# Block-sparse attention and a squared-ReLU MLP in one kernel: the second batch by gathered blocks, more transposes on TensorE, w_in products for pairs of token tiles

## The chip, the cores and the metric

The kernel runs on one core of a Trainium2 chip. The metric is the device time of one execution in microseconds, lower is better. The engines are TensorE (PE; its weight loads are listed apart as PEld), VectorE (DVE), ScalarE (ACT), GpSimd (POOL) and SyncE (SP), which in this kernel does nothing but issue DMAs. Each engine runs its own instructions in the order in which they stand; a semaphore makes one wait for another.

## The reference

Attention over 4 batches, 8 heads, 768 positions of 64 numbers, with a mask by blocks of 32 positions: each of the 24 query blocks sees its neighbours, the first and the last block, and three random blocks of its own; the first and last query block see everything. What comes out, 3072 tokens of 512 numbers, goes through a layer of 2048 with a squared ReLU:

```python
scores = scale * np.matmul(q, k.transpose(0, 1, 3, 2))
mask = np.abs(blk_i - blk_j) <= 1
mask = mask | (blk_i == 0) | (blk_j == 0) | (blk_i == 23) | (blk_j == 23)
for qb in range(24):
    for kb in sampled_blocks[qb]:       # three blocks a row
        mask[qb*32:(qb+1)*32, kb*32:(kb+1)*32] = True
attn = softmax(np.where(mask, scores, -1e9))
x = np.matmul(attn, v).transpose(0, 2, 1, 3).reshape(3072, 512)
r = np.maximum(x @ w_in, 0.0)           # 512 x 2048
return (r * r) @ w_out                  # 2048 x 512
```

Inputs and output are float32. The kernel casts to bf16 for TensorE.

## The kernel before

**Two ways of attention.** A unit is a pair of heads of one batch, 16 in all, four to a batch. Batches 0 and 1 (`SB = 2`) are dense: `attend` takes a unit and 256 queries, in three steps of 256 keys. Each step is `scores` (line 343, on TensorE), `exps` (line 357, one exponential of 128x1024 on ScalarE) and, for most, `masks` (line 363, a product on VectorE with a 0/1 tile `MK` which `mask_tile` and `mask_evac` build on TensorE and VectorE). For the first 256 queries of batch 0 there is no product: TensorE adds rows of minus infinities to the scores (`add` in line 343). Then come `values` or `values_full` (lines 372 and 389) and `normalize` (line 406).

Batches 2 and 3 are sparse. A `visit` (line 887) takes 128 query positions of all eight heads, as two groups of 64, and looks only at the blocks that the groups see. It needs the keys of the random blocks gathered in SBUF (`k_gather`, line 584: copies on POOL or VectorE whose addresses are block numbers in registers), and the values of those blocks gathered from a copy in DRAM: `v_store` (line 537) writes one batch's values as rows, `v_gather` (line 574) reads them back, through an indirect DMA on POOL or DMAs with register addresses on SP, and `v_window` (line 544) reads the neighbours and the edge blocks. Then `s_scores`, `s_exps` (line 620), `s_masks` (line 626), `s_values` (line 632; its matmuls stand at line 653 and go by column halves of TensorE, 128x64), and `s_normalize` (line 656). Two visits make 256 tokens.

A table tells which blocks to gather: `table_places`, `table_slots` (line 475) and `table_rows` build it on POOL and VectorE, `table_masks` makes the masks `MKS` of the gathered blocks, and `load_blocks` (its loads are line 561) brings block numbers into registers of POOL, VectorE and SP, all in one place.

**Transposes.** TensorE wants queries and keys, and later the attention's output, with the 64 or 128 features on the partitions. Queries and keys of batch 0 are transposed on TensorE (`transp`, copied out of PSUM by `evac`), those of the other batches by a transposing DMA on SP (`transp_dma`, line 311). The outputs of batch 0 go over TensorE (`x_transp`, `x_evac`), those of batch 1 and of the visits by DMA (lines 440 and 666).

**The MLP.** Twelve tiles of 256 tokens (`xT`, features on the partitions, `XT_BUFS = 4` in SBUF). For each, four times: `hidden` (line 681) multiplies four chunks of 128 of `w_in` with 256 tokens in four parts of eight matmuls; `relu` (line 697, ScalarE or VectorE), `square` (line 713, ScalarE, POOL or VectorE) follow. `output` (line 736) multiplies the squares with `w_out`, 512 wide; `out_copy` and `store` bring the result to DRAM.

**Halves of TensorE.** Nearly all matmuls have 64 rows of weights, one half of the array. `pair` (lines 201 to 203) issues two, one for each row half, which run together:

```python
def pair(out, lhsT, rhs, crossed=False, **kw):
    for r, rows in enumerate(HALVES):
        last = nc.tensor.matmul(out(r ^ crossed), lhsT(r ^ crossed, rows), rhs(r ^ crossed, rows), skip_group_check=True, **kw)
    return last.ins
```

Every such matmul is line 203 of the profile, so its groups are told apart by their tiles: `X<-xT,w_in_sb` is `hidden`, `X<-w_out_sb,g` is `output`, `X<-QKT` and `X<-QKT,KG` are scores, `X<-VB,pT` are values. `X` is PSUM, four slots of 128x2x512 (`NX = 4`).

**The order.** Each step above is a task, numbered as it is created. A table of words, `PROGRAM` (line 1001), lists all 1224 in the order in which they are issued, each with the engine that gets it (P, V, A, G for POOL, S) and, for a task that takes a PSUM slot, the slot: `P463/2` would be task 463 on TensorE into slot 2. `run_program` (line 92) goes through it; buffers are handed out in turn. So the order on each engine is written out by hand in that table and nothing reorders it.

**Loads.** `load` (line 145) brings a unit's queries, keys and values to raw buffers (three for queries, two each for keys and values), through SP, behind a gate on the weights' arrival. `cast_qk` and `cast_v` make bf16 of them; copies and casts of all engines are line 123.

## Time and profile before

| | us |
|---|---|
| three runs: lowest, median, highest | 261.82, 262.56, 263.5 |
| the profiled execution | 258.88 |
| its span on the core (first to last work) | 257.1 |
| granted clock of TensorE, mean | 1.00 |
| DMA: bytes moved, mean rate | 47.08 MB, 183 GB/s |
| POOL: squares (line 720), 20 of | 31.6, mean 1.587 each |
| POOL: indirect gathers of values (line 579), 19 of | 20.2, mean 1.061 each |
| ScalarE: ReLU (line 707), 28 of | 29.8, mean 1.068 each |
| VectorE: ReLU (line 709), 20 of | 24.5, mean 1.224 each |

The page of the profile gives for each engine the time in which it did work; register loads, semaphores and DMA issues are not counted in it. The groups of a line and a tile follow, with the busy time of all, the mean of one in ns, and the idle time just before them with what ended it. The profiled execution is 3.68 us shorter than the median of the three runs (1.4%), and 2.94 shorter than the lowest of them; where times are taken apart below, it is that execution.

Line numbers are those of the kernel before. In the changed kernel the same operations stand lower: the register loads at 580 for 561, copies at 125 for 123, the store of values at 557 for 538, the window's DMAs at 571 and 575 for 552 and 556, the indirect gathers at 598 for 579, the key gathers at 612 to 618 for 593 to 599, the squares at 754 for 720.

### The profile page before, as it was taken

How to read it: one execution, taken by the hardware profiler on the slowest of the kernel's cores; microseconds unless marked ns; L12 is line 12 of the kernel's file. 1: busy time of each engine (PE TensorE's matmuls, PEld its weight loads, DVE VectorE, ACT ScalarE, POOL GpSimd, SP SyncE). 2: the span in 40 equal slices, each digit the busy share in tenths (PEclk: the TensorE clock that was granted, in tenths of full speed). 3: DMA queues.
4: the chain of work that ended last, by engine and by line, in shares of the span. 5: the costliest groups of instructions: out<-in, count | busy, mean ns of one | idle time of the engine just before them, and what ended most of it. 6: DMA issues, size and time to landing. Idle time of an engine off the chain costs nothing.

```text
span 257.1 us, 12061 instructions
## 1 busy us (share of the span) xinstructions
PE 243.1 (95%) x5265; PEld 182.1 (71%) x5265; DVE 171.3 (67%) x408; ACT 183.6 (71%) x217; POOL 98.8 (38%) x178
## 2 busy tenths in 40 slices
...
GB/s 200 374 250 207 206 205 155 270 202 252 250 281 179 197 202 153 340 229 154 188 243 202 194 174 167 251 214 199 129 206 95 189 40 60 5 121 148 23 86 83
DMA packets 64692, 47.08 MB, mean 183 GB/s; under 512 B 31567, under 2 KB 60624, under 8 KB 64640
## 3 DMA queue, kind: packets, MB, share of 16 engines
...
## 4 chain that ended last, share of the span: by engine, by line
PE 53%; DVE 5%; DVEq 1%; issue 1%; ACT 1%; ACTq 0%
PE X L203 49%; PE X L653 4%; DVE VB L123 1%; ACT pT L623 1%; DVEq L561 1%; DVE MKS L123 1%; DVE pT L630 1%; DVE r L709 0%; DVE KG L599 0%; DVE qc L123 0%; DVE XS L413 0%; DVE KG L593 0%; DVE XS L662 0%; DVEq L599 0%; DVE rs L410 0%
## 5 line engine op out<-in xcount | busy, mean ns | idle before, releaser
L203 PE MATMUL X<-xT,w_in_sb 64*128 64x256 bf16 x1536 | 100.8, 269 | 2.8 <-issue 1.5
L203 PE MATMUL X<-w_out_sb,g 64*128 64x512 bf16 (+3 forms) x960 | 95.2, 334 | 0.1
L203 PEld LDWEIGHTS <-w_in_sb 64*128 64x128 bf16 x1536 | 74.6, 94 | 16.0 <-issue 5.4
L360 ACT ACTIVATE pT<-X 128x1024 bf16<-128x1024 f32 x72 | 70.6, 1030 | 7.6 <-PE X L203 6.8
L623 ACT ACTIVATE pT<-X 128x768 bf16<-128x768 f32 (+1 forms) x56 | 41.6, 766 | 26.5 <-PE X L203 23.9
L203 PEld LDWEIGHTS <-g 64*128 64x128 bf16 x960 | 40.3, 94 | 26.3 <-PE X L203 0.4
L720 POOL TENSOR_TENSOR g<-r 128x1024 bf16<-128x1024 f32 (+1 forms) x20 | 31.6, 1587 | 64.4 <-ACT r L707 47.2
L707 ACT ACTIVATE r<-X 128x1024 f32<-128x1024 f32 x28 | 29.8, 1068 | 20.6 <-PE X L203 20.5
L709 DVE TENSOR_SCALAR r<-X 128x1024 f32<-128x1024 f32 x20 | 24.5, 1224 | 26.7 <-PE X L203 13.7
L367 DVE TENSOR_TENSOR pT<-pT,VG 128x1024 bf16<-128x1024 bf16 x60 | 40.9, 715 | 0.2
L718 ACT ACTIVATE g<-r 128x1024 bf16<-128x1024 f32 (+1 forms) x40 | 35.2, 899 | 2.7 <-DVE r L709 2.5
L203 PE MATMUL X<-QKT 64*128 64x256 bf16 (+1 forms) x384 | 31.6, 250 | 3.3 <-DVE XS L413 1.3
L630 DVE TENSOR_TENSOR pT<-pT,MKS 128x768 bf16<-128x768 bf16 (+1 forms) x48 | 27.6, 607 | 10.7 <-ACT pT L623 10.5
L203 PEld LDWEIGHTS <-QKT 64*128 64x128 bf16 x384 | 16.7, 95 | 9.5 <-issue 4.1
L579 POOL DMA_INDIRECT VG<-rows,idx x19 | 20.2, 1061 | 4.4 <-issue 2.6
L203 PEld LDWEIGHTS <-pT 64*128 64x128 bf16 x768 | 16.0, 94 | 1.9
L203 PE MATMUL X<-VB,pT 64*128 64x65 bf16 x768 | 17.1, 190 | 0.0
L203 PEld LDWEIGHTS <-KG 64*128 64x128 bf16 x528 | 13.8, 95 | 4.5 <-issue 0.2
L659 DVE RECIPROCAL ss<-X 128x8 f32<-128x8 f32 x12 | 2.5, 206 | 19.5 <-PE X L653 17.3
L653 PEld LDWEIGHTS <-pT 128*64 128x64 bf16 x624 | 11.9, 111 | 4.9 <-issue 3.7
L203 PE MATMUL X<-QKT,KG 64*128 64x64 bf16 x528 | 15.3, 190 | 0.1
L123 POOL CAST VB<-vs 128x768 bf16<-128x768 f32 x9 | 7.8, 869 | 16.5 <-DMA vs<-in_v_dram 16.4
(107 smaller groups left out, 210.3 us busy)
## 6 DMA issues: line engine op xcount, KB each, us to landing
...
```

What stands on the lines that cost most here:

```text
L123: (V if e == "DVE" else G).tensor_copy(out=out, in_=in_)
L203: last = nc.tensor.matmul(out(r ^ crossed), lhsT(r ^ crossed, rows), rhs(r ^ crossed, rows), skip_group_check=True, **kw)
L360: A.activation(out=pT[:, :, 0:n], in_=stile.pop(a)[:, :, 0:n], func=AF.Exp, scale=scale)
L367: V.tensor_tensor(out=pT, in0=pT, in1=m[:, None].broadcast_to([P, 2, len(cs), w]), op=AOP.mult)
L579: G.indirect_dma_start(out=to[0:RS * HB], out_offset=None, in_=pairs, in_offset=bass.IndirectOffsetOnAxis(ap=idx[0:RS * HB, g - 1:g], axis=0))
L623: A.activation(out=pT[:, :, 0:n], in_=stile.pop((u, v, gs))[:, :, 0:n], func=AF.Exp, scale=scale)
L630: V.tensor_tensor(out=pT, in0=pT, in1=m[:, None].broadcast_to([P, 2, n]), op=AOP.mult)
L653: nc.tensor.matmul(po[i * D:(i + 1) * D, h, a * VW:(a + 1) * VW], pts[g][:, h, c * D:(c + 1) * D], val, start=a == 0 and c == 0, stop=c == ...
L707: A.activation(out=to, in_=src, func=AF.Relu)
L709: V.tensor_scalar(out=to, in0=src, scalar1=0.0, scalar2=None, op0=AOP.max)
L718: A.activation(out=g, in_=r, func=AF.Square)
L720: (G if e == "POOL" else V).tensor_mul(out=g, in0=r, in1=r)
```

## The change

Five things change together.

Batch 1 is sparse too (`SB` 2 to 1): six visits more, 18 in all, and a third store of values as rows. Only batch 0 is dense, and all of its scores get their mask by rows added on TensorE (`MASKED = ()`, `attend(a, True)`); the mask tiles, their building and the products of line 363 are gone.

Queries and keys of batch 1 (`BY_PE`, units 4 to 7) are transposed on TensorE. The outputs of all visits are too: `s_transp` now writes into the free end of the PSUM slot that held the visit's values, and a new task `s_evac` copies it to the x tile on VectorE or ScalarE.

The tiles 3 to 10, counted from 0 (`PAIRED = (3, 11)`), go through `hidden` in pairs: two chunks of `w_in` with 512 moving columns from two neighbouring x tiles, for four chunks with 256. ReLU, square and the squares' buffers are shared by the two tiles; the number of tasks per tile pair halves. The `w_out` products stay by one tile.

The table of blocks is cut into five tasks (`table_ids`, `table_dup`, `table_near`, `table_drawn`, `table_low`), with its scratch in the output buffers `ys`, cleared by POOL, and `load_blocks` into two for each engine: blocks of groups 0 to 3 and of 4 on.

`PROGRAM` is a new list, 1194 words.

```diff
-    SB, VR, KG_BUFS, VG_BUFS = 2, D + 2, 2, 3
+    SB, VR, KG_BUFS, VG_BUFS = 1, D + 2, 2, 3
...
+    PAIRED = (3, 11)
+    BY_PE = range(HP, 2 * HP)
-    MASKED = ((256, 512), (512, 768), (0, 256))
+    MASKED = ()
...
-    ... many("xT", XT_BUFS, [P, HP, QW])
+    ... many("xT", XT_BUFS // 2, [P, 2, HP, QW])
...
+            at = (xb[b, c0].at + PAIRED[0]) % XT_BUFS
+            xT[b, c0] = XTP[at // 2][:, at % 2]
+            xpair[b, c0] = XTP[at // 2]
...
+        low[0] = table_scratch()[-1]
+        G.memset(low[0], 0.0)
...
-        load_blocks("POOL")
-        load_blocks("DVE")
-        load_blocks("SP")
...
-    def load_blocks(e):
-        for g in wanted[e]:
+    def load_blocks(g0, g1, e):
+        for g in [g_ for g_ in wanted[e] if g0 <= g_ < g1]:
             if g not in held_at[e]:
                 held_at[e][g] = blocks_of(g, ENGINE[e])
...
-    def s_transp(b, v, e):
-        sy.dma_start(out=x_tile(b, v // 2 * QW)[:, :, v % 2 * P:v % 2 * P + P], in_=xtile.pop(("s", b, v)).rearrange("p a h d -> p (a h d)"), transpose=True)
+    def s_transp(b, v, buf, e):
+        xs = xtile.pop(("s", b, v))
+        pt = tile_of(buf)[:, :, 384:512].bitcast(BF).rearrange("p r (a i) -> p r a i", i=D)
+        for a in range(HP):
+            for r, rows in enumerate(HALVES):
+                nc.tensor.transpose(pt[:, r, a], xs[rows, a].rearrange("p h d -> p (h d)"), identb[rows, rows])
+        xtile["t", b, v] = pt
+
+    def s_evac(b, v, e):
+        to = x_tile(b, v // 2 * QW)[:, :, v % 2 * P:v % 2 * P + P]
+        copy(e, to.rearrange("q a (r i) -> q r a i", r=2), xtile.pop(("t", b, v)))
...
+    MATES = {}
+    for i, T in enumerate(TILES):
+        if not PAIRED[0] <= i < PAIRED[1]:
+            MATES[T] = [T]
+        elif (i - PAIRED[0]) % 2 == 0:
+            MATES[T] = TILES[i:i + 2]
     def per_unit(T):
-        return NU_
+        return 4 // len(MATES[T])
...
+        x = xT[b, c0][:, None] if z == 1 else xpair[b, c0]
...
-            hlast[T, f] = pair(lambda i: htile[T, f][:, i, j * w:(j + 1) * w],
+            hlast[T, f] = pair(lambda i: htile[T, f][:, i, j * z * w:(j + 1) * z * w],
                                lambda i, rows: w_in_sb[rows, kc, (f + i * n + j) * P:(f + i * n + j + 1) * P],
-                               lambda i, rows: xT[b, c0][rows, kc], crossed,
+                               lambda i, rows: x[rows, :, kc], crossed,
...
-                x = T_(transp_dma, u, w, deps=[c] + old_s, put=[qc])
+                if u in BY_PE:
+                    hb = Buf("X")
+                    t = T_(transp, u, w, ALL, hb, deps=[c], get=[hb], put=[qc])
+                    x = T_(evac, u, w, ALL, deps=[t] + old_s, put=[hb])
+                else:
+                    x = T_(transp_dma, u, w, deps=[c] + old_s, put=[qc])
...
-        nm = T_(s_normalize, b, v, deps=[va], get=[xs], put=[yb, ot])
-        mu["s", b, v] = T_(s_transp, b, v, deps=[nm] + x_get(b, v // 2 * QW), put=[xs])
+        nm = T_(s_normalize, b, v, deps=[va], get=[xs])
+        xt = T_(s_transp, b, v, yb, deps=[nm], put=[xs])
+        mu["s", b, v] = T_(s_evac, b, v, deps=[xt] + x_get(b, v // 2 * QW), put=[yb, ot])
...
+    i_ = tb["ids"] = T_(table_ids, deps=[t, p])
+    for e_ in ("POOL", "DVE", "SP"):
+        T_(load_blocks, 0, 4, deps=[i_])
+        T_(load_blocks, 4, nb, deps=[i_])
...
-            attend(a, us[0] < HP and a[1] == 0)
+            attend(a, True)
...
     PROGRAM = """
-        A29 G35 P4/3 V32 P30/0 P12/2 P14/3 P9/1 P5/1 V31 P33/1 V111 P36/3 P0/2 A37 V1 V34 P102/2 V209 V46 P47/0 P106/1 A103 V48 P104/3
+        P11/0 P5/1 P15/2 V259 S18 P0/3 A36 S35 G42 P43/0 V1 G100 A39 G53 P288 P37/1 V44 V38 P54/2 P40/3 A55 P17/0 G61 A41 P91/1 G74
...
```

**The register loads on VectorE.** Before, VectorE at about 97 us: masks of gathered blocks (`MKS`), the row numbers `idx`, the register loads (`tab`, the count behind it), and the normalize of batch 1's outputs (`rs`, `XS`), with the dense mask products (`pT`, `VG`) around them.

```order
L367 TENSOR_TENSOR pT_87<-pT_87,VG_208 128x1024
L123 CAST MKS<-X_147 128x5x64 x3
L123 CAST MKS<-X_147 128x6x64 x3
L524 TENSOR_SCALAR idx<-X_147,lane 128x11
L561 TENSOR_LOAD tab x6
L410 RECIPROCAL rs<-X_148 128x4
L413 TENSOR_TENSOR XS<-X_148,rs 128x2x2x64
L367 TENSOR_TENSOR pT_86<-pT_86,VG_208 128x1024
L367 TENSOR_TENSOR pT_89<-pT_89,VG_208 128x1024
L367 TENSOR_TENSOR pT_91<-pT_91,VG_208 128x1024
L367 TENSOR_TENSOR pT_88<-pT_88,VG_208 128x1024
```

After, VectorE in the middle of batch 0's attention: the end of one of the table's tasks (`dup`), then the loads in two pieces between the normalize steps of batch 0 (`rs`, `xq`), the copies of its outputs to the x tile (`xT`) and a ReLU (`r`):

```order
L504 TENSOR_SCALAR dup<-dup 11x8
L125 COPY QKT<-X_147 128x2x4x64
L412 RECIPROCAL rs<-X_148 128x4
L415 TENSOR_TENSOR xq_114<-X_148,rs 128x2x2x64
L580 TENSOR_LOAD tab x4
L412 RECIPROCAL rs<-X_146 128x4
L415 TENSOR_TENSOR xq_111<-X_146,rs 128x2x2x64
L125 COPY xT_115<-X_146 128x2x2x64
L580 TENSOR_LOAD tab x2
L743 TENSOR_SCALAR r_83<-X_147 128x1024
```

The six loads moved from behind the masks `MKS` to places ahead of two outputs of batch 0 (`xq_111` and the ReLU `r_83`).

**SP around the first store of values as rows.** Before, in batch 1, the loads stood between transposing DMAs of queries and keys (`QKT<-qc`) and stores of results, with the store of batch 2's values (`rows`) three places behind and the first windows (`VG<-rows`) after two more transposes:

```order
L312 DMA_TRANSPOSE QKT<-qc_108 128x6x128
L561 TENSOR_LOAD tab x3
L149 DMA vs_79<-in_v_dram 128x2x384
L771 DMA out_dram<-ys_84 128x1024
L312 DMA_TRANSPOSE QKT<-qc_109 128x6x128
L538 DMA rows_70<-VB_189 128x3168
L771 DMA out_dram<-ys_85 128x1024
L149 DMA vs_80<-in_v_dram 128x2x384
L312 DMA_TRANSPOSE QKT<-qc_106 128x6x128
L552 DMA VG_207<-rows_70 16x2x1056 x2
L556 DMA VG_207<-rows_70 64x528 x2
```

After, the first store is that of batch 1's values; one register load stands ahead of it, four behind the first window, and there are only plain loads between:

```order
L151 DMA vs_81<-in_v_dram 128x2x384
L580 TENSOR_LOAD tab
L153 DMA qs_77<-in_q_dram 128x6x128
L153 DMA qs_75<-in_q_dram 128x6x128
L557 DMA rows_70<-VB_190 128x3168
L153 DMA ks_78<-in_k_dram 128x6x128
L571 DMA VG_206<-rows_70 16x2x1056 x2
L575 DMA VG_206<-rows_70 64x528 x2
L580 TENSOR_LOAD tab x4
L151 DMA vs_80<-in_v_dram 128x2x384
```

The store and the first window now have one load of keys between them, and the four register loads hold the loads of batch 2's values instead of batch 3's neighbours in the queue.

**POOL up to the first gathers.** Before, POOL loaded its five block numbers between casts (`VB`, `qc`) and squares (`g`) in batch 1, and then copied keys (`KG`):

```order
L123 CAST VB_189<-vs_80 128x2x6x64 x2
L720 TENSOR_TENSOR g_94<-r_83 128x1024
L123 CAST VB_189<-vs_79 128x2x6x64
L561 TENSOR_LOAD tab x5
L123 CAST qc_109<-qs_76 128x384 x2
L720 TENSOR_TENSOR g_98<-r_81 128x1024
L593 COPY KG_119<-QKT 128x4x64
L596 COPY KG_119<-QKT 128x4x2x8
L597 COPY KG_119<-QKT 128x4x2x8
```

After, it first clears the table's scratch (`ys`), loads four block numbers, casts (`qc`, `VB`) and squares once; then come the rest of the casts of batch 1's keys, queries and values, two loads of `w_in`, and the fifth block number:

```order
L125 CAST qc_109<-ks_79 128x384 x2
L125 CAST VB_190<-vs_81 128x2x6x64
L330 DMA w_in_sb<-in_moe_w_in_dram 128x4x512
L754 TENSOR_TENSOR g_96<-r_83 128x512
L330 DMA w_in_sb<-in_moe_w_in_dram 128x4x512
L125 CAST VB_190<-vs_80 128x2x6x64
L125 CAST qc_107<-qs_75 128x384 x2
L125 CAST qc_108<-ks_79 128x384 x2
L580 TENSOR_LOAD tab
L125 CAST VB_190<-vs_81 128x2x6x64
L754 TENSOR_TENSOR g_97<-r_84 128x1024
L612 COPY KG_118<-QKT 128x4x64
```

All five loads and the casts stand in the list among batch 0's attention, and the first key gather at its end; before, loads and gather stood among that of batch 1.

## The prediction

> **What bounds the kernel now.** I read the page first, then busy times by stage, then the chain of waits, then the pieces on TensorE. The page, and the time by stage (columns: stretch, its length, then busy us and pieces of PE, PEld, DVE, ACT, POOL, the granted clock, the DMA share, GB/s):
> ```profile
> PE 243.1 (95%) x5265; PEld 182.1 (71%) x5265; DVE 171.3 (67%) x408; ACT 183.6 (71%) x217; POOL 98.8 (38%) x178
> ...
> 0.00:10.00 10.00, 7.16 (x113) 4.92 (x115) 6.84 (x24) 5.02 (x6) 2.39 (x14) 1.00 0.82 260
> 10.00:50.00 40.00, 38.07 (x821) 30.99 (x821) 34.05 (x71) 38.91 (x47) 17.69 (x29) 1.00 1.09 223
> 50.00:95.00 45.00, 44.12 (x994) 32.84 (x992) 41.91 (x96) 41.51 (x45) 9.98 (x15) 1.00 1.12 233
> 95.00:125.00 30.00, 27.55 (x666) 22.44 (x663) 24.07 (x62) 20.59 (x25) 18.98 (x31) 1.00 0.94 197
> 125.00:150.00 25.00, 23.27 (x538) 17.51 (x539) 15.21 (x45) 17.84 (x22) 12.41 (x27) 1.00 0.95 211
> 150.00:250.00 100.00, 99.72 (x1988) 70.39 (x1986) 48.46 (x113) 59.41 (x75) 37.36 (x63) 1.00 0.59 134
> 250.00:257.10 7.10, 3.22 (x168) 2.98 (x165) 0.72 (x2) 0.27 (x1) 0.00 (x0) 1.00 0.23 76
> ```
> TensorE is the bound over the whole. It is not busy for 14.0 us (257.1 - 243.1), and the stages say where: 2.84 in the first ten, 1.93 from 10 to 50, 0.88 from 50 to 95, 2.45 and 1.73 from 95 to 150, 0.28 in the next hundred, 3.88 at the end. From 10 to 50 it is ScalarE that is full (38.91 of 40), and from 50 to 95 ScalarE and VectorE together (92% and 93%); TensorE keeps pace there. After 150 nothing but TensorE counts. So other engines can give back at most what lies before 150.

> **TensorE's own work.** Five pieces give its pitch, the time from one pair of row halves to the next (columns: start, us from first start to last end; x is the count; the groups after them give the mean ns of one, behind the busy time):
> ```profile
> 228.77 1.04 PE L203 MATMUL X<-xT,w_in_sb 64*128 64x256 bf16 x16
> 227.04 1.89 PE L203 MATMUL X<-w_out_sb,g 64*128 64x512 bf16 x16
> 123.36 0.52 PE L203 MATMUL X<-QKT,KG 64*128 64x64 bf16 x24
> 96.48 0.53 PE L203 MATMUL X<-VB,pT 64*128 64x65 bf16 x24
> 148.81 0.88 PE X L653 x48
> ...
> L203 PE MATMUL X<-xT,w_in_sb 64*128 64x256 bf16 x1536 | 100.8, 269 | 2.8 <-issue 1.5 <-ACT pT L623 0.5 <-DMA xT<-XS 0.4
> L203 PE MATMUL X<-w_out_sb,g 64*128 64x512 bf16 x704 | 87.5, 376 | 0.0
> L203 PE MATMUL X<-VB,pT 64*128 64x65 bf16 x768 | 17.1, 190 | 0.0
> L203 PE MATMUL X<-QKT,KG 64*128 64x64 bf16 x528 | 15.3, 190 | 0.1
> L653 PE MATMUL X<-VG,pT 128*64 128x65 bf16 x528 | 13.1, 197 | 0.9 <-issue 0.6 <-ACT pT L623 0.3
> ```
> Take the last piece's own length off and divide by the pairs left: (1.04-0.269)/7 = 0.110 us for a pair 256 wide, (1.89-0.376)/7 = 0.216 for 512, (0.52-0.19)/11 = 0.030 for 64, 0.031 for 65, and (0.88-0.197)/47 = 0.0145 for each of line 653.
> Removed with the dense second batch: 72 pairs of scores (7.9 us), 288 pairs of values (8.9) and the 9 pairs that build masks (1.0), 17.8 in all. Added: mask rows on 48 pairs of batch 0's scores (5.3), 132 pairs against gathered keys (4.0), 24 pairs of the edge blocks' scores (0.7), 312 matmuls of line 653 (4.5), 48 pairs of transposes of queries and keys (1.4) and 72 of outputs (2.2), taken at the 64-wide pitch: 18.1. The w_in products of eight tiles become 256 pairs of 512 for 512 pairs of 256: 55.3 for 56.3. Sum of TensorE's work: **-0.7 us** (bounds -1.0 and +0.5, if strided pairs of 512 miss the pitch of w_out). The change does not shorten the bound; it can only take out waits.

> **ScalarE and VectorE** (columns as in the groups above):
> ```profile
> L360 ACT ACTIVATE pT<-X 128x1024 bf16<-128x1024 f32 x72 | 70.6, 1030 | 7.6 <-PE X L203 6.8
> L623 ACT ACTIVATE pT<-X 128x768 bf16<-128x768 f32 x48 | 38.0, 811 | 21.8 <-PE X L203 19.7 <-PE X L653 1.9
> L623 ACT ACTIVATE pT<-X 128x384 bf16<-128x384 f32 x8 | 3.8, 492 | 4.6 <-PE X L203 4.2 <-issue 0.5
> L367 DVE TENSOR_TENSOR pT<-pT,VG 128x1024 bf16<-128x1024 bf16 x60 | 40.9, 715 | 0.2
> L630 DVE TENSOR_TENSOR pT<-pT,MKS 128x768 bf16<-128x768 bf16 x40 | 23.3, 613 | 10.7 <-ACT pT L623 10.5
> ```
> ScalarE loses 36 dense exponentials (37.1 us) and gains 24 + 4 gathered ones (19.5 + 2.0): -15.6. VectorE loses all 60 mask products (42.9) and gains 20 + 4 of line 630 (about 14.6), so some -28. Neither counts after 150. Where they count:
> The start. Until batch 0's attention is done ScalarE sets the pace, and its 36 exponentials there (37.1 us) are the same as before. VectorE loses masks and gains the table of slots and its register loads. I take 0, with bounds -1.5 (VectorE's masks gone from exponential to values) and +3 (the table work and the first gathers fall into the same stretch).
> The dense stage. TensorE's 0.88 us not busy from 50 to 95 mostly go: -0.7 (0 to -0.9).

> **The register loads.** A row of the chain of waits (start, us, what), and the pieces around it (idle time before a piece, and its releaser, in brackets):
> ```profile
> 99.20 0.86 DVEq L561
> ...
> 97.39 1.05 PE L203 MATMUL X<-xT,w_in_sb 64*128 64x256 bf16 x16 [0.38 <-DMA xT<-XS]
> 100.21 0.18 DVE L410 RECIPROCAL rs<-X 128x4 f32<-128x4 f32 x1 [2.66 <-ACT pT L360]
> 100.91 0.39 PE L203 MATMUL X<-QKT 64*128 64x256 bf16 x4 [1.02 <-DVE XS L413]
> ```
> Six loads of block numbers into VectorE's registers (line 561) hold its queue; the last ends at 100.06. VectorE idles 2.66 us though the input of what follows is long there, the normalize behind them is late, and TensorE waits 0.38 and 1.02. The new order puts four and two of them into the start. Behind the four stands the normalize of unit 1's second query tile, which TensorE transposes some 3 us of its work after it computes it; behind the two, the second relu of the first x tile. POOL has four and one, in front of casts of batch 1's keys and values; SP has one and four, in front of loads. Gain -1.4 (0, if they only move the wait, to -2.45, all that stage has).

> **Visits.** Six more visits come, 18 for 12. What of 95 to 150 is left, 2.45 - 1.4 + 1.73 = 2.8 us, falls on four visits, 0.70 each; the eight after 150 have 0.28, 0.035 each. The dear ones lie where a batch's gathers start beside loads and casts of the next. I take 0.70 for the first visit of batches 1 and 2, and 0.035 for sixteen (batch 3's first, in the cheap stage, shows no more): 2.0 for 3.1, **-1.1**. Bounds: twelve visits at 0.70 give +5.5, all at 0.035 give -2.5. A change from row halves to column halves at line 653 costs too:
> ```profile
> PEld L653 <- issue: 3.7, 11, 0.7
> ```
> that is 0.34 us for each of 11, not all of it on the path; the 0.9 us of TensorE's own over 12 visits are 0.08. For six visits +0.5 to +2.1; I take the middle, +1.2 (my estimate).

> **Transposes.** What waited for the normalized outputs, and the two kinds of issue on SP:
> ```profile
> PE X L203: 1.8, 4
> L666 SPq DMA_TRANSPOSE xT<-XS x12: 1190/1210/1827, 132.4 to 227.7; - x12
> 63.28 0.53 SPq L149 DMA_DIRECT2D vs<-in_v_dram  x1
> ```
> TensorE waited 1.8 us for outputs; 1.02 of it is counted above, so 0.8 is left for transposes on TensorE to save: -0.8 (0 to -0.8). Each of 26 DMA transposes that go also frees SP 1.2 us, where a plain load holds it 0.53; SP is not waited for after 150, so nothing is counted. In their place 18 + 8 copies out of PSUM come on VectorE and ScalarE, some 0.5 us each, under TensorE's cover (0 in the sum; if it fails, they are in the visits' upper bound).
> [...]

> Sum: -0.7 + 0 - 0.7 - 1.4 - 1.1 + 1.2 - 0.8 = **-3.5 us**. The profiled execution took 258.88 us (1.8 around its span) and lies 3.7 under the median of the runs, 262.56; the difference is put on the median: 262.56 - 3.5 = 259.1. Start and end stay.

> **Rivals.**
> Nothing moves (20%). TensorE's work is the same, and the relieved engines hardly held it up: only 0.88 us from 50 to 95. If register loads cost as much in the start and the visits keep their old mean, -0.7 + 1.2 is left: 263.1. For it: ScalarE's 38.91 of 40 in the start, where each displaced microsecond shows. Against it: VectorE's 28 us less.
> Transposes were hidden (8%): the waits at outputs come from late normalizes, not from the DMA, and stay. Then -3.5 + 0.8: 259.9, no change to measure. For it: one wait of 0.38 names the DMA, the others VectorE. [...]
> The gathers of batch 1 come too late (17%), and it is slower. Before, the store of a batch's values went out at 104.10, and the first rows could be fetched only 6.2 us later; the gather then lands after 4.2:
> ```profile
> 104.10 0.59 SPq L538 DMA_DIRECT2D rows<-VB  x1
> ...
> 110.27 0.80 SPq L552 DMA_DIRECT2D VG<-rows  x2
> DMA to landing us min/median/max: 3.5/4.2/6.0
> ```
> that is 10.4 us and POOL's issue. In the new order TensorE has about 13 us of work, by the pitches above, between the place of POOL's last cast of batch 1's values and that batch's first line 653. With more than 2 us of delay on POOL or SP there, TensorE stands still; behind the waiting matmuls lie the w_out products of the first tile. To get there POOL passes five register loads, two squares, two weight loads and eight casts of batch 1 after its part of the table; three squares, a weight load and a key gather follow before its first row gather. Six microseconds late would cost 4 at the first visit, and as much at the next two together: 259.1 + 8 = 267.1; it decides from about 6 us (slower by over 1%).

> **How the numbers follow.** About 1% (2.6 us) is what a measurement of this kernel tells from no change. The forecast has 55%: 46 under 259.9, and 9 that stay within 1%. Nothing moves: 19 within, 1 slower. Transposes hidden: 8 within. Gathers late: 16 slower, 1 within. So faster 46%, same 37%, slower 17%. The forecast's own range is 256 to 261. All lower bounds together are -8.7, or 253.9; I take 254 as the low end. At the top I go to 266, into the late gathers, and leave out their worst.

> **What would show it.** TensorE's pieces: a pair of w_in at 0.216; line 653 18 times, with no idle over 0.7 before one. ScalarE full (over 95%) from 10 to 50 as before, and under 85% from 55 on. No idle of VectorE over 2 us behind register loads while TensorE waits. TensorE's time not busy: about 5 us up to 50, under 3 from 50 to 200, 4 at the end. It is wrong if the first visit of batch 1 waits over 1 us for VG, if the start is longer than before by 2 us, or if POOL's squares end waits of w_out products.

## The result, and the profile after

The changed kernel takes 272.75 us (median of four runs, 271.07 to 273.67); the kernel before took 262.19 (259.03 to 263.5) beside it. The ratio is 1.0437 (95% interval 1.0325 to 1.0550): slower, outside the range of the prediction, and faster was the likeliest case there. In this document a time is the median of all runs of a kernel, while a ratio leaves out runs that are over 1.5% above the kernel's fastest; the profiled executions of e1_stores and f2_single are such runs.

First the page of the profile after (each engine's busy time, and the DMA queue that brings instructions), from an execution of 272.52 us with a span of 270.8:

```profile
PE 247.6 (91%) x4975; PEld 160.7 (59%) x4975; DVE 159.0 (59%) x402; ACT 175.1 (65%) x218; POOL 126.0 (47%) x241
...
q8 instruction: 39, 0.64, 1.0%
```

VectorE and ScalarE have less to do than before (159.0 for 171.3, 175.1 for 183.6), as forecast, though by less than the 28 and 15.6 us that were to go, since copies out of PSUM, among others, came in their place; TensorE is idle for 23.2 us instead of 14.0. Busy times by stage of the kernel after (columns as in the prediction: stretch, length, PE, PEld, DVE, ACT, POOL, granted clock, DMA share, GB/s):

```profile
0.00:25.00 25.00, 20.54 (x384) 15.55 (x386) 16.72 (x51) 18.91 (x24) 11.57 (x34) 1.00 0.98 252
25.00:40.00 15.00, 14.18 (x334) 12.03 (x331) 7.58 (x19) 14.14 (x19) 7.25 (x11) 1.00 1.08 281
40.00:70.00 30.00, 25.01 (x705) 22.04 (x698) 25.22 (x67) 22.29 (x29) 18.26 (x36) 1.00 1.05 248
70.00:82.00 12.00, 9.33 (x155) 5.86 (x150) 6.45 (x20) 5.27 (x7) 6.18 (x12) 0.86 0.92 174
82.00:150.00 68.00, 67.46 (x1347) 40.14 (x1340) 45.11 (x116) 47.27 (x60) 41.42 (x83) 1.00 0.94 217
150.00:225.00 75.00, 72.68 (x1395) 40.28 (x1390) 46.89 (x116) 52.42 (x64) 34.26 (x62) 1.00 0.56 140
263.40:270.80 7.40, 0.03 (x2) 0.00 (x0) 0.20 (x1) 0.27 (x1) 0.00 (x0) 0.66 0.45 143
```

and the same stretches of the kernel before, its end from 253.3 on:

```profile
40.00:70.00 30.00, 29.37 (x686) 24.56 (x684) 26.01 (x48) 28.47 (x33) 7.92 (x15) 1.00 1.13 234
70.00:82.00 12.00, 12.00 (x257) 7.49 (x254) 11.08 (x31) 11.94 (x13) 5.27 (x10) 1.00 1.04 227
82.00:150.00 68.00, 63.56 (x1484) 48.96 (x1481) 52.10 (x140) 49.49 (x58) 31.39 (x58) 1.00 0.99 207
150.00:225.00 75.00, 74.79 (x1582) 52.91 (x1580) 43.89 (x108) 48.55 (x60) 33.55 (x60) 1.00 0.68 146
253.30:257.10 3.80, 0.00 (x0) 0.00 (x0) 0.29 (x1) 0.18 (x1) 0.00 (x0) 1.00 0.13 37
```

From 40 to 82 TensorE was busy for 41.4 of 42 us, now for 34.3. Busy time still hides waits between matmuls that overlap (one 256 wide lasts 269 ns in the profile, and the next pair begins 110 behind it), so a second measure is used from here on, the **lost time** of a stretch: its length less the work of the matmuls that begin in it, each taken at about half of the prediction's pitch per pair (64 rows by 256 columns 54.5 ns, by 512 107.8, by 64 or fewer 14.5 and so on; 15.2 for line 653, now 672). All work together is 226.4 us before and 226.5 after. Lost:

| us | 0–25 | 25–40 | 40–70 | 70–82 | 82–150 | 150–225 | 225 to TensorE's end | behind it |
|---|---|---|---|---|---|---|---|---|
| before | 10.0 | 1.7 | 1.5 | 0.2 | 9.3 | 3.2 | 1.0 | 3.8 |
| after | 11.0 | 2.1 | 8.0 | 4.7 | 4.1 | 6.5 | 0.5 | 7.3 |

So 11.1 us were lost anew from 40 to 82, 3.5 at the end, 3.3 from 150 to 225 and 1.3 before 40; 5.2 were won from 82 to 150, where the prediction had looked for its gain. The rows where TensorE stands still (start, us, piece, idle time before it and its releaser) in the kernel after:

```profile
6.88 0.45 PE L307 MATMUL X<-identb,qc 64*128 64x64 bf16 x10 [1.70 <-POOL qc L125]
...
37.83 0.23 PE L429 MATMUL X<-identb,xq 64*128 64x64 bf16 x4 [0.76 <-DVE xq L415]
44.06 0.23 PE L429 MATMUL X<-identb,xq 64*128 64x64 bf16 x4 [1.23 <-DVE xq L415]
55.69 0.26 PE L307 MATMUL X<-identb,qc 64*128 64x64 bf16 x6 [0.87 <-DVE qc L125]
...
69.34 0.22 PE L672 MATMUL X<-VB,pT 128*64 128x65 bf16 x1 [0.65 <-issue]
77.46 0.23 PE L205 MATMUL X<-QKT,KG 64*128 64x64 bf16 x3 [2.67 <-issue]
78.71 1.96 PE L205 MATMUL X<-xT,w_in_sb 64*128 64x256 bf16 x16
```

Up to 56 it waits for POOL and VectorE. The longest stop, 2.67 us at 74.8, has no releaser that the profile shows and falls in the middle of a group of twelve alike (nine before it, three behind). The stages there by microsecond (columns as above):

```profile
74.00:75.00 1.00, 0.79 (x15) 0.39 (x11) 0.02 (x1) 1.00 (x3) 1.00 (x6) 1.00 1.08 250
75.00:76.00 1.00, 0.00 (x0) 0.00 (x0) 0.85 (x2) 0.65 (x1) 1.00 (x3) 1.00 0.48 152
76.00:77.00 1.00, 0.00 (x0) 0.00 (x0) 1.00 (x2) 0.00 (x0) 0.86 (x2) 1.00 0.12 34
77.00:78.00 1.00, 0.54 (x9) 0.35 (x11) 1.00 (x5) 0.28 (x1) 0.98 (x1) 1.00 0.01 4
78.00:79.00 1.00, 1.00 (x10) 0.53 (x8) 0.55 (x6) 0.53 (x1) 0.08 (x1) 0.50 0.42 108
```

The weight loads stop too (0.00 busy from 75 to 77), the DMA queues, full until then, drain (1.08, 0.48, 0.12), and half a microsecond after work resumes the granted clock is 0.50, for 3.4 us (78.0 to 81.4 in the clock records): the w_in piece at 78.71 takes 1.96 us where 16 of its kind took 1.04 in the kernel before.

At the end, SyncE's queue of the kernel after issues the stores of the last results:

```profile
263.63 0.35 SPq L811 DMA_DIRECT2D out_dram<-qs  x1
264.08 0.38 SPq L811 DMA_DIRECT2D out_dram<-ys  x1
264.51 1.49 SPq L814 DMA_DIRECT2D out_dram<-ys  x3
266.06 0.58 SPq L816 DMA_DIRECT2D out_dram<-ys  x1
266.74 0.39 SPq L811 DMA_DIRECT2D out_dram<-qs  x1
```

The store of an earlier tile in four pieces (lines 814 and 816, 2.1 us) stands between the parts of the last tile, and the very last store is issued 3.3 us after TensorE's end.

### The profile page after: what moved, and what is told of

The parts are those of the page before. It is cut to its first block, busy times and chain, and to the rows that moved or that the text cites. A ratio compares the mean times of both kernels' runs of the same rounds, so it can differ in the third digit from the quotient of the medians.

```text
span 270.8 us, 11663 instructions
## 1 busy us (share of the span) xinstructions
PE 247.6 (91%) x4975; PEld 160.7 (59%) x4975; DVE 159.0 (59%) x402; ACT 175.1 (65%) x218; POOL 126.0 (47%) x241
## 4 chain that ended last, share of the span: by engine, by line
PE 74%; ACT 9%; issue 4%; DVE 3%; DMA 3%; POOL 2%; SPq 2%; DVEq 0%; ACTq 0%
PE X L205 64%; PE X L672 7%; ACT pT L642 3%; DMA ys<-in_v_dram 3%; ACT g L752 2%; SPq L171 2%; PE X L400 2%; ACT r L741 2%; ACT pT L362 1%; DVE r L743 1%; PE X L689 1%; POOL VB L125 1%; DVE qc L125 1%; POOL w_out_sb L333 1%; ACT QKT L123 1%
## 5 line engine op out<-in xcount | busy, mean ns | idle before, releaser
L205 PE MATMUL X<-xT,w_in_sb 64*128 64x512 bf16 (+1 forms) x1024 | 97.8, 325 | 1.0 <-ACT QKT L123 0.4
L642 ACT ACTIVATE pT<-X 128x768 bf16<-128x768 f32 (+1 forms) x84 | 62.7, 766 | 40.6 <-PE X L205 36.4
L205 PEld LDWEIGHTS <-w_in_sb 64*128 64x128 bf16 x1024 | 48.9, 95 | 25.8 <-issue 1.9
L754 POOL TENSOR_TENSOR g<-r 128x1024 bf16<-128x1024 f32 (+1 forms) x22 | 33.5, 1527 | 58.3 <-ACT r L741 53.1
L649 DVE TENSOR_TENSOR pT<-pT,MKS 128x768 bf16<-128x768 bf16 (+1 forms) x72 | 43.0, 627 | 19.2 <-ACT pT L642 19.0
L752 ACT ACTIVATE g<-r 128x1024 bf16<-128x1024 f32 (+1 forms) x34 | 33.4, 984 | 11.8 <-DVE r L743 11.5
L362 ACT ACTIVATE pT<-X 128x1024 bf16<-128x1024 f32 x36 | 35.3, 1029 | 3.4 <-PE X L205 3.3
L741 ACT ACTIVATE r<-X 128x1024 f32<-128x1024 f32 x28 | 30.2, 1086 | 10.7 <-PE X L205 10.5
L205 PE MATMUL X<-QKT 64*128 64x256 bf16 (+1 forms) x288 | 22.3, 235 | 0.4 <-ACT pT L362 0.2
L672 PEld LDWEIGHTS <-pT 128*64 128x64 bf16 x936 | 18.1, 111 | 7.5 <-issue 6.0
L618 POOL COPY KG<-QKT 128x64 int32 x90 | 20.5, 275 | 0.0
L672 PE MATMUL X<-VG,pT 128*64 128x65 bf16 x792 | 19.6, 197 | 1.0 <-issue 0.5
L205 PE MATMUL X<-R,oh 64*128 64x256 bf16 x144 | 18.3, 277 | 0.0
L618 DVE COPY KG<-QKT 128x64 int32 x108 | 18.3, 239 | 0.0
L678 DVE RECIPROCAL ss<-X 128x8 f32<-128x8 f32 x18 | 3.7, 204 | 19.5 <-PE X L672 16.7
```

The source lines that it names most:

```text
L362: A.activation(out=pT[:, :, 0:n], in_=stile.pop(a)[:, :, 0:n], func=AF.Exp, scale=scale)
L618: eng.tensor_copy(out=rows[:, :, :, r_ * w:(r_ + 1) * w], in_=src[:, :, :, bass.ds(at[r_] * w, w)])
L642: A.activation(out=pT[:, :, 0:n], in_=stile.pop((u, v, gs))[:, :, 0:n], func=AF.Exp, scale=scale)
L649: V.tensor_tensor(out=pT, in0=pT, in1=m[:, None].broadcast_to([P, 2, n]), op=AOP.mult)
L672: nc.tensor.matmul(po[i * D:(i + 1) * D, h, a * VW:(a + 1) * VW], pts[g][:, h, c * D:(c + 1) * D], val, start=a == 0 and c == 0, stop=c == ...
L741: A.activation(out=to, in_=src, func=AF.Relu)
```

## The experiments

All times are set against runs of the kernel before on the same chip, made together with them; that kernel itself took 256 to 262 us from one group of runs to another (a group is what shares a time in the column "before"), so kernels of one group are compared first. Lost times are of one profiled execution each; besides the columns, f4_dmaout loses 14.0 from 225 to TensorE's end.

| kernel | time | before | ratio (95%) | span | lost to 40 | 40–82 | 82–150 | 150–225 | behind TensorE |
|---|---|---|---|---|---|---|---|---|---|
| before | 262.19 | | | 257.1 | 11.8 | 1.6 | 9.3 | 3.2 | 3.8 |
| after | 272.75 | 262.19 | 1.0437 (1.0325–1.0550) | 270.8 | 13.1 | 12.7 | 4.1 | 6.5 | 7.3 |
| e1_stores | 270.01 | 261.29 | 1.0272 (1.0161–1.0384) | 269.0 | 12.3 | 13.8 | 5.1 | 6.6 | 4.0 |
| e2_start | 272.01 | 261.29 | 1.0473 (1.0378–1.0567) | 269.1 | 13.9 | 10.1 | 5.0 | 5.9 | 7.1 |
| e3_table | 274.20 | 261.29 | 1.0523 (1.0444–1.0601) | 272.9 | 12.7 | 14.8 | 4.5 | 6.7 | 7.1 |
| e4_loads | 269.58 | 261.29 | 1.0385 (1.0291–1.0478) | 266.3 | 14.6 | 7.2 | 5.3 | 5.0 | 7.1 |
| f1_loads | 266.25 | 257.18 | 1.0335 (1.0264–1.0406) | 264.7 | 14.0 | 11.3 | 3.2 | 4.6 | 4.6 |
| f2_single | 272.93 | 257.18 | none | 270.3 | 14.0 | 10.7 | 8.0 | 6.0 | 4.0 |
| f3_dmaqk | 277.97 | 257.18 | 1.0825 (1.0763–1.0887) | 275.6 | 12.9 | 18.2 | 8.7 | 5.8 | 4.4 |
| f4_dmaout | 300.86 | 257.18 | 1.1614 (1.1524–1.1704) | 296.6 | 13.6 | 6.6 | 16.6 | 17.1 | 4.3 |
| g1_nops | 271.51 | 256.63 | 1.0579 (1.0486–1.0673) | 268.9 | 12.5 | 14.2 | 2.9 | 5.0 | 7.2 |
| g2_orders | 264.93 | 256.63 | 1.0326 (1.0256–1.0397) | 263.7 | 13.9 | 10.3 | 4.0 | 3.9 | 4.6 |
| g3_table_loads | 266.66 | 256.63 | 1.0405 (1.0331–1.0480) | 265.5 | 12.8 | 10.4 | 3.8 | 3.9 | 7.4 |
| g4_start_cut | 264.63 | 256.63 | 1.0321 (1.0262–1.0380) | 262.3 | 12.1 | 11.4 | 3.8 | 3.9 | 4.1 |
| h1_shift | 273.44 | 262.24 | 1.0379 (1.0324–1.0434) | 272.5 | 14.4 | 9.6 | 5.5 | 8.3 | 7.2 |
| h2_wout | 266.72 | 262.24 | 1.0196 (1.0123–1.0269) | 263.8 | 13.5 | 8.4 | 5.8 | 5.0 | 4.0 |
| h3_wout_loads | 268.80 | 262.24 | 1.0223 (1.0174–1.0273) | 267.7 | 12.8 | 11.6 | 5.2 | 6.2 | 4.6 |
| h4_wout_cut | 266.80 | 262.24 | 1.0147 (1.0110–1.0185) | 265.4 | 12.5 | 10.6 | 5.4 | 5.7 | 4.1 |
| k1_three | 263.10 | 256.33 | 1.0273 (1.0199–1.0347) | 261.4 | 12.5 | 10.0 | 3.9 | 3.9 | 4.0 |
| k2_keys | 262.06 | 256.33 | 1.0250 (1.0185–1.0314) | 259.5 | 12.5 | 8.1 | 3.9 | 4.0 | 4.1 |

### One wait at a time

**e1_stores** moves the word of the four-piece store ahead, to where its data are ready.

```diff
-        P1169 S1125 P1158 P1159
+        P1169 S1125 S1115 P1158 P1159
...
-        P10/0 S1115 S1193
+        P10/0 S1193
```

> One word of the order moved: the store of the tenth x tile's result (four DMAs on SP) from behind the three stores of the last tile to ahead of them. If the order on SP set the end: TensorE ends as before the edit (263.4 in the changed kernel), the last DMA on SP is issued at about 264.9 instead of 266.74, the time after TensorE's end falls from 7.3 to about 5, the span from 270.8 to 268.4, the time by 2.4. Rival, the end is set by how long the last bytes take to land whatever their order: span 270.8, no change.

SyncE's queue of this kernel:

```profile
259.13 1.38 SPq L814 DMA_DIRECT2D out_dram<-ys  x3
260.55 1.04 SPq L816 DMA_DIRECT2D out_dram<-ys  x1
...
266.08 0.39 SPq L811 DMA_DIRECT2D out_dram<-qs  x1
```

Behind TensorE's end (264.9) 4.0 us are left for 7.3, so the place of that store cost 3.3 us (4.0 to 4.6 are left in every kernel with this edit, 7.1 to 7.4 in every one without it). The span fell by 1.8 only, because 40 to 82 lost 1.1 more in this execution; the loss in the middle varies by that much between executions (g1_nops below).

**e2_start** gives unit 0's scores their turn ahead of the transposes of unit 1's queries, which wait for POOL; the copy of these (word 55) goes from ScalarE to VectorE, and two of TensorE's idle pieces (words 5 and 15) move behind the scores.

```diff
-        P11/0 P5/1 P15/2 V259 S18 P0/3 ... V38 P54/2 P40/3 A55 P17/0 ... P93/0 P51/2 V64
+        P11/0 V259 S18 P0/3 ... V38 P40/3 P5/2 P15/2 P17/0 ... P93/0 P54/2 V55 P51/2 V64
```

> Only the order of the first 7 us: the transposes of the second unit's queries and their copy go behind the first unit's first two score tasks, and two of the idle matmuls go from the very start into the gap before those scores. If the order at the start cost what the trace shows: first exponential at about 6.5 for 8.33, pairs of 256 at 0.11 us from about 6 us on and not from 9.7, TensorE's lost time up to 25 us 9.2 for 11.0, span 269.3. Rival, VectorE's work from 40 to 60 sets the pace and takes the gain back: lost time up to 40 falls, that from 40 to 60 grows by as much, span 270.8 within 0.5.

The first clock record, of 1.00, begins at 7.0 us (9.7 after, 5.5 before), and pairs 256 wide begin 0.11 us apart from 7.1 on, 0.21 ahead of it; but the first 25 us lose only 0.5 less, and 25 to 40 lose 1.3 more, which some kernels without this edit do as well (e4_loads, h1_shift). The start is a cause of little.

**e3_table** leaves out three steps of the table (`table_near`, `table_drawn`, `table_low`), so that VectorE has time for the normalize steps and casts behind them; the blocks that are gathered are then not those of the reference.

```diff
     def table_near(e):
+        return
...
-        G.memset(low[0], 0.0)
+        G.memset(low[0], 1.0)
```

> Left out: the part of the table that works out the masks and the row numbers of the gathered blocks (16 small operations on VectorE, 7.6 us between 35.7 and 46.3); the table's scratch is filled with ones, so masks and rows are the same for all. If a full VectorE holds TensorE up from 40 to 60: its lost time there falls from 5.6 to about 3 us, span about 268. Rival, TensorE waits there for loads, casts on POOL or key copies that come no earlier: lost time from 40 to 60 still 5 us or more, span 270.8 within 0.7.

The stops of TensorE from 40 to 75:

```profile
52.09 0.72 PE L205 MATMUL X<-xT,w_in_sb 64*128 64x256 bf16 x10 [1.10 <-issue]
58.84 0.34 PE L307 MATMUL X<-identb,qc 64*128 64x64 bf16 x6 [2.68 <-issue]
65.58 0.61 PE L205 MATMUL X<-xT,w_in_sb 64*128 64x256 bf16 x8 [1.13 <-issue]
74.02 0.22 PE L675 MATMUL X<-VB,pT 128*64 128x65 bf16 x1 [3.44 <-issue]
```

The waits for `xq` and `qc` are gone, and nothing is won: there are 8.4 us of stops without a releaser, and two stretches at half clock (granted 0.50 from 58.3 and from 75.4). That VectorE's lateness had covered these stops is not shown by this run alone. Such stops (of 0.4 us and more, 30 to 100 us) add to 7.4 us in e1_stores and 6.2 in g1_nops below, which run the kernel after's work in this stretch, against 3.3 in the profiled execution of the kernel after; so they differ that much between executions.

**e4_loads** cuts the four loads that arrive about 70 us to 8 of their 128 partitions; batch 2 computes with stale rows there.

```diff
+        n = 8 if (u, w) in ((9, 2), (10, 0), (10, 1), (11, 1)) else P
-            sy.dma_start(out=..., in_=(qv, kv, vv)[w][b, a])
+            sy.dma_start(out=...[0:n], in_=(qv, kv, vv)[w][b, a][0:n])
```

> Left out: 15 sixteenths of four loads of batch 2 (values of unit 9, queries and keys of unit 10, keys of unit 11), which are issued on SP from 62.05 to 77; the rest of the raw buffers keeps old data. If TensorE's 2.67 us without a named wait at 74.8 come from its program being fetched late behind a full DMA backlog (the fetch of 16 KB ran at 74.8 to 76.0): the DMA share falls under 1 from 68 to 74, that fetch comes by about 71, no stop over 1 us there, no half clock from 78 to 81.4, span 266.5 to 267.5. Rival, the stop is a wait for key copies on POOL or VectorE: it stays over 2 us, span 270.8 within 0.7.

```profile
70.00:82.00 12.00, 12.00 (x259) 8.34 (x255) 6.87 (x20) 8.97 (x12) 7.84 (x19) 1.00 0.41 86
```

That stretch of e4_loads has TensorE busy throughout at full clock, with the DMA share 0.41 for 0.92. One execution doesn't settle it, since e1_stores and g1_nops, with the loads whole, have no stop at that place either (theirs come earlier, and from 70 to 82 they lose 3.0 and 4.6). Over all kernels it holds better: from 70 to 82 the six with these loads cut lose 0.1 to 1.9 us, and those with the loads whole 1.0 to 5.8 (f2_single to f4_dmaout left aside).

### Parts of the change undone, with the store of e1_stores moved

**f1_loads** issues four loads of batch 2 earlier, and the last load of w_out right behind the one before it.

```diff
-        P273/3 S261 V217 ... G86 A279 A264 S402 P265/3 ... S401 ... S424 ... S410
+        G85 G86 P216 ... P273/3 S402 S401 S424 S410 S261 V217 ...
```

> With the store moved as in e1_stores; besides, four loads of batch 2 (keys and values of unit 8, queries of unit 11, values of unit 9) stand ahead of the first window on SP, behind which SP sat idle from 45.4 to 52.3 while the DMA share fell to 0.74, and the third w_out load follows the second at once on POOL. Nothing is left out. If TensorE starves for code behind the DMA backlog between 58 and 75: the backlog is over some 5 us earlier, no stop over 2 us and no half clock from 55 to 85, span 264 to 266 (e1_stores has 269.0). Rival, the same bytes queue ahead of the gathers or of the code all the same: a stop of over 2 us and half clock remain, span 268 to 270.

The span is 4.3 less than e1_stores', but on a chip where the kernel before is faster too, and the ratio is no better (1.0335 for 1.0272). Stops of 2.07 and 1.83 us before 60.38 and 73.38, and a half-clock stretch (the w_in piece at 61.54 takes 1.89 us, its like at 65.45 1.05), remain: moving these loads doesn't remove them.

**f2_single** makes all products with w_in by one tile again.

```diff
-    PAIRED = (3, 11)
+    PAIRED = (12, 12)
```

> With the store moved as in e1_stores; the pairing of tiles is undone: tiles 3 to 10 go through their w_in products one by one, 256 wide, in the same places of the order. If pairing neither gains nor loses on the path: TensorE's work 1.0 us more, the span 269 to 271 against 269.0 of e1_stores, lost time from 150 to 225 still over 6 us. Rival, pairing holds TensorE up after 150, since a unit needs two x tiles and its ReLU and squares stand for two: lost time from 150 to 225 falls to 3.5 or less and the span to 266 or 267.

The four times lie between 266.58 and 278.4 and give no interval: inconclusive. In the profiled execution 95 to 125 loses 6.3 us where e1_stores loses 2.1, 4.6 of it in three stops of the kind that is explained below; 40 to 82 loses 3.1 less; the spans are 270.3 and 269.0. That the pairing has a part in the slowdown is not shown, nor is it excluded.

**f3_dmaqk** transposes batch 1's queries and keys by DMA again, **f4_dmaout** the visits' outputs.

```diff
-    BY_PE = range(HP, 2 * HP)
+    BY_PE = ()
```
```diff
-        xt = T_(s_transp, b, v, yb, deps=[nm], put=[xs])
-        mu["s", b, v] = T_(s_evac, b, v, deps=[xt] + x_get(b, v // 2 * QW), put=[yb, ot])
+        mu["s", b, v] = T_(s_transp, b, v, deps=[nm] + x_get(b, v // 2 * QW), put=[xs])
```

> With the store moved as in e1_stores; queries and keys of batch 1 are transposed by DMA on SP, as before the change, at the places where TensorE did it, and their copies out of PSUM are gone. If the casts in front of these transposes and VectorE's and ScalarE's copies hold TensorE up from 40 to 60: its lost time there falls from 7.1 (e1_stores; 5.6 in the changed kernel) to 4 or less, span 266. Rival, the eight DMA transposes, 1.2 us each on SP and more in the full DMA, come too late: loads and first windows behind them slip by up to 10 us, TensorE waits more from 40 to 82, span 271 to 276.

> With the store moved as in e1_stores; the outputs of the visits are transposed by DMA on SP, as before the change; the transposes on TensorE (2.2 us of its work) and 18 copies of 0.5 us on ScalarE and VectorE are gone. If those copies hold up the exponentials and squares after 150: lost time from 150 to 225 falls from 6.6 to 4, and the span by 3 to 5, to 264 to 266. Rival, the DMA transposes arrive late behind gathers and w_in products wait for them: lost time from 82 to 225 grows, span 269 to 272.

Against e1_stores, of another group, the span is 6.6 and 27.6 us longer; against f1_loads of the same group, which has its loads moved besides, the time is 11.7 and 34.6 longer. Two rows of f3_dmaqk, where TensorE waits in turn for the table and for a transposing DMA (VectorE, which writes the table's `ys`, had itself waited 8.28 us for such a DMA):

```profile
50.66 0.90 PE L543 MATMUL X<-identb,ys 64*128 64x11 bf16 x5 [5.83 <-issue]
...
67.72 0.51 PE L205 MATMUL X<-QKT 64*128 64x64 bf16 x12 [1.86 <-DMA QKT<-qc]
```

In this order both parts earn their place by far; undoing either without a new order shows what the order relies on, not what the part would cost in the old one.

### What the stops without a releaser are

**g1_nops** was to put 64 empty instructions ahead of TensorE's `warm` matmuls at the start. They did not reach its program (4975 matmuls and 39 packets of code, as in the kernel after), so it is the kernel after once more. **g2_orders** joins the edits of e1, e2 and f1 and leaves nothing out; **g3_table_loads** joins e3 and e4, **g4_start_cut** e1, e2 and e4.

```diff
+    for _ in range(64):
+        nc.tensor.nop()
     for _ in range(N_WARM):
```

> The changed kernel with 64 empty instructions on TensorE ahead of its first matmul, nothing else. In the runs so far TensorE stopped without a named wait after its matmuls number 991, 1119, 1247, 1374 and 1502, 128 apart, which is 256 instructions or one fetch of 16 KB, and each stop ended 2.3 to 2.9 us after a fetch began. If these are the borders of fetched blocks, all stops between 40 and 90 us that have no named wait move 32 matmuls ahead, to numbers 959, 1087, 1215, 1342 and 1470 (give or take 1); their sum need not change, span 268 to 273. Rival, they are waits of certain matmuls for data: they stay after 1119, 1247, 1374 or 1502.

> The three edits of order together (the store as in e1_stores, the start as in e2_start, the loads and w_out as in f1_loads); nothing is left out. If the places are independent: 264.7 (f1_loads) less the 1.4 by which e2_start ended TensorE earlier, span 263 to 264, still 6 us above the kernel before. Rival, an earlier TensorE only meets its code or VectorE sooner: span 264.7 or more.

> Left out: both the table arithmetic of e3_table and the loads of e4_loads. To be held against e4_loads (span 266.3, lost from 40 to 60 us 4.57), where TensorE was not stopped by late code from 70 on. If VectorE's full queue holds TensorE up from 37 to 60: lost time from 25 to 60 falls from 8.2 to 5 or less, span 263 to 264. Rival, what VectorE gives free is taken by late code at the next borders: lost time from 25 to 70 stays within 1 us of e4_loads' 10.4, span 266 or more.

> Left out: the loads of e4_loads; besides the store as in e1_stores and the start as in e2_start. If the three places add up: 266.3 less 2.7 to 3.3 at the end and 1 to 1.4 at the start, span 262 to 263, and what is left above the kernel before (257.1) is lost between 25 and 70 and after 150. Rival, the earlier start is taken back by code or VectorE: span 263.5 or more.

The kernel after takes 271.51 here. Moved words alone (g2_orders) take back 6.6 us of its 14.9, dropping the table's steps and loads 4.9, the start, the store and the loads 6.9. Without table and loads, 25 to 70 still loses 11.3, where e4_loads lost 10.4: again the loss stayed, now in other stops.

The stops without releaser have a pattern. Counting TensorE's matmuls from the start and looking up when the DMA records show a 16 KB packet of the instruction queue begin (both my own counts from the traces):

```
kernel      stop ends, us   idle   after matmul   packet began   before the end of the stop
after       69.34           0.65   1374           67.0           2.3
after       77.46           2.67   1502           74.8           2.6
e1_stores   59.17           2.68   1119           56.5           2.6
e1_stores   67.01           2.17   1247           64.6           2.4
g1_nops     59.55           2.41   1119           57.1           2.4
g1_nops     73.36           2.35   1374           70.5           2.8
e3_table    58.84           2.68   1119           56.2           2.6
e3_table    74.02           3.44   1374           71.2           2.9
g2_orders   59.89           2.43   1119           57.5           2.4
k2_keys     53.09           1.61    991           50.6           2.5
```

The numbers lie 128 apart (a record or two short later on): 128 matmuls with their weight loads are 256 instructions, and 39 packets with 0.64 MB (the page's row above) are 16 KB each. The page's 4975 matmuls and as many weight loads are 38.9 times 256, for 39 packets; the 5265 of the kernel before are 41.1 times 256, for 41. By that a packet is 256 of TensorE's instructions, 64 bytes each. In these rows TensorE stops at the end of such a block of its program and goes on 2.3 to 2.9 us after the next block's transfer begins; a stop is 0.65 to 3.44 us long. It doesn't stop at every border, and in the kernel after and g1_nops, which run the same work, not at the same ones.

**h1_shift** tests it: 38 matmuls of 16 columns come ahead of the `warm` matmuls at the start and six of these go, 32 more in all, so that the same work stands 32 places later in the program.

```diff
+    for _ in range(19):
+        pair(lambda i: X[NX - 1][:, i, 0:16], lambda i, rows: warm[rows, 0:P], lambda i, rows: warm[rows, 0:16], start=True, stop=True)
-    for _ in range(N_WARM):
+    for _ in range(N_WARM - 3):
```

> The changed kernel with 38 short idle matmuls (16 columns) ahead of its first work and 6 of the long idle ones left out, 32 more in all, which is 64 instructions, a quarter of a fetch. If TensorE's stops without a named wait are the borders of fetched code: counted from the first matmul they stay after numbers 991, 1119, 1247, 1374 and 1502 (give or take 1), which is 32 matmuls earlier in the work. Rival, they are waits for data: they come at the same work as before, after numbers 1151, 1279, 1406 and 1534. The time is not told apart by this: 268 to 273.

```profile
47.55 0.27 PE L205 MATMUL X<-xT,w_in_sb 64*128 64x256 bf16 x1 [0.94 <-issue]
48.88 0.35 PE L309 MATMUL X<-identb,qc 64*128 64x64 bf16 x12 [0.43 <-ACT QKT L123]
53.75 0.33 PE L205 MATMUL X<-VB,pT 64*128 64x65 bf16 x10 [1.45 <-issue]
69.15 0.20 PE L205 MATMUL X<-QKT,KG 64*128 64x64 bf16 x2 [0.74 <-issue]
76.36 0.23 PE L691 MATMUL X<-identb,XS 64*128 64x64 bf16 x3 [2.19 <-issue]
```

The stops without releaser stay behind matmuls 863, 991, 1375 and 1502 of the new count, and so fall on other work (the last on `XS`, where the kernel after had `QKT,KG`); the wait for ScalarE's `QKT` stays with its work and comes behind matmul 889, 32 later than in e3_table and g2_orders (857). At 1119 and 1247 this execution doesn't stop for 0.4 us or more. That shows the borders to be those of the code. The time is near the kernel after's of the other groups (273.44; 272.75 and 271.51).

### What holds the code back

**h2_wout** moves w_out's last two loads from 52 and 59 us to about 39 (with e1 and e2; nothing left out), **h3_wout_loads** adds f1's four loads ahead, **h4_wout_cut** e4's cut to h2.

```diff
-        P798/0 G82 P8/3 ... V286 G85 P216 ... S26 G86 A279
+        P798/0 G82 G85 G86 P8/3 ... V286 P216 ... S26 A279
```

> The store as in e1_stores, the start as in e2_start, and the last two w_out loads on POOL moved from 52 and 59 us to right behind the last w_in load at 39 us; nothing is left out. To be held against g2_orders (263.7). If the packets of these two loads, which filled the DMA engines at 53 to 57 and 62 to 67 us, make the code late: the fetches for the borders 1119 and 1247 start over 60 matmuls ahead of them, no stop over 1 us at either, lost time from 40 to 70 falls from 8.3 to 5 or less, span 260 to 262. Rival, other transfers take their place: stops over 1 us at 1119 or 1247 and half clock remain, span 263 or more.

> h2_wout with four loads of batch 2 ahead of the first window on SP as in f1_loads; nothing is left out. If the DMA queue ahead of the code is all that counts: the stretch from 45 to 52, in which SP sat idle, takes the loads, the stop at 1374 and 1502 goes as well, span 259 to 261. Rival, the loads now stand ahead of the first gathers, which come later: line 672's first matmuls wait, span not under h2_wout's.

> h2_wout with the four loads of batch 2 cut to a sixteenth, as in e4_loads (left out). If both kinds of transfers make the code late, none over 1 us is left from 50 to 85, no half clock, and the span is 258 to 260, what is left over the kernel before being VectorE's and ScalarE's waits. Rival, code is late without them too, since narrow matmuls use a block up in less time than a fetch takes: stops of over 1 us remain at two borders or more, span 261 or more.

```profile
53.76 0.72 PE L205 MATMUL X<-xT,w_in_sb 64*128 64x256 bf16 x10 [0.58 <-issue]
...
75.27 0.23 PE L205 MATMUL X<-QKT,KG 64*128 64x64 bf16 x3 [0.65 <-issue]
```

In h2_wout no stop without releaser is over 0.65 us, and none is followed by half clock (granted 1.00 from 40 to 82). The time is 4.5 us over the kernel before, the least of all that leave nothing out, and 6.7 less than h1_shift in the same group. The two profiled spans differ by 8.7; of these, 3.2 lie at the end, which is e1's word, 3.3 from 150 to 225, where no edit is aimed, 0.9 before 40 and only 1.2 from 40 to 82 (8.4 for 9.6; e2_start alone has 10.1): the long stop is gone, most of the loss there stayed. What the loads of w_out are worth by themselves is not separated, as no kernel with e1's and e2's edits alone was run. In the kernel after w_out's packets, the last of which begins at 68.2 us, share the DMA engines with batch 2's loads and the first gathers, which begin at 57.7 (DMA share 1.12 from 60 to 70); before, the last packet of the weights began at 43.7 us and the first window was read at 110 (the row in the prediction).

The same loads brought forward (h3) win nothing more, nor does cutting them (h4). Both have instead one wait of TensorE, 2.76 and 2.63 us before about 48, for a copy on VectorE. VectorE and POOL of h3_wout_loads there:

```profile
44.35 3.13 DVE L528 CAST ys<-ys 11x32 bf16<-11x32 f32 x1
...
47.66 0.16 DVE L528 CAST ys<-ys 11x32 bf16<-11x32 f32 x1
```
```profile
44.77 0.82 POOL L125 CAST VB<-vs 128x768 bf16<-128x768 f32 x1
45.56 1.88 POOL L754 TENSOR_TENSOR g<-r 128x1024 bf16<-128x1024 f32 x1
```

A cast of 11 rows of 32 took 3.13 us, and 0.16 a little later; it ended at 47.48, with POOL's square (47.44), and the copy for TensorE came behind it. h4_wout_cut has the same cast at 3.58 us, ending within 0.05 us of the square. That VectorE stood still until POOL's cast and square were done is my reading of these ends.

**k1_three** is h2 with the cuts of e3 and e4; **k2_keys** lets batch 1's key gathers copy six fixed blocks in one instruction besides, for six of one each.

```diff
+        if b == SB:
+            eng.tensor_copy(out=rows[:, :, :, 0:RS * w], in_=src[:, :, :, 0:RS * w])
+            return
```

> h2_wout (nothing at the end, the start or the w_out loads left to gain) with the table arithmetic of e3_table and 15 sixteenths of four loads of batch 2 left out. If several chains of about the same length lie side by side from 25 to 70 us (VectorE's table, code behind w_out, loads), each alone hidden by the others: with all three shortened the lost time there falls from 10.8 (h2_wout) to 6.5 or less, span 259 or less. Rival, one further chain sets the pace, casts, transposes and key copies for the first visits: 9.5 or more stay, span 262 or more.

> k1_three, and for batch 1 one copy of six fixed blocks of keys in place of six copies by block number (72 copies of about 0.25 us on VectorE and POOL become 12 longer ones; the keys are those of other blocks). If key copies are on the path between 50 and 80: lost time from 40 to 82 is 1.5 us or more less than in k1_three. Rival, they lie beside TensorE's work: within 0.7 of k1_three.

From 40 to 82 k2_keys loses 1.9 us less than k1_three. That the key copies were on the path does not follow: both stop 2.76 us at the same border, and only k1_three runs 3.4 us at half clock behind it (its w_in piece at 61.00 takes 1.89 us, its like at 64.60 1.05; k2_keys has a granted clock of 1.00 from 40 to 82). Two stops of k2_keys that are left:

```profile
53.09 0.72 PE L206 MATMUL X<-xT,w_in_sb 64*128 64x256 bf16 x10 [1.61 <-issue]
59.28 0.27 PE L308 MATMUL X<-identb,qc 64*128 64x64 bf16 x6 [2.76 <-issue]
```

With VectorE relieved of all this, the three blocks of code from matmul 735 on take 6.5, 6.5 and 6.2 us, and hold 5.1, 4.4 and 3.2 us of work (each the sum of the pitches of 128 matmuls): here code arrives at about one block in 6.4 us while the DMA engines are full (share 1.04 to 1.20 in the 2 us before each of their packets, my sum over the DMA records). It is no fixed figure. From 40 to 75 us the next block's packet begins only after TensorE has entered the block ahead of it: 3.9 to 4.2 us after at these three borders, 2.3 to 5.5 in the kernel after, 1.8 to 3.5 in the kernel before, and 0.6 and 1.7 behind the third of these borders, where the share had fallen to 0.31 and 0.25; some 2.3 us at least come on top until work goes on. In the kernel before, no block from 35 to 99 us holds less than 4.8 us of work; in the kernel after six clearly do, the least 3.2 and 3.8, since scores, values and transposes on gathered blocks take 15 ns a matmul. Still 40 to 70 loses 8.0, as in the kernel after, and the kernel stays 5.7 us over the one before.

## Why the prediction was wrong

**The step that failed** is "The change does not shorten the bound; it can only take out waits." The first half held: work of TensorE +0.1 us for -0.7, within its bounds, and a w_in product of 512 costs what a w_out product does (groups of the kernel after; x, busy, mean ns of one, idle before):

```profile
L205 PE MATMUL X<-w_out_sb,g 64*128 64x512 bf16 x704 | 87.6, 379 | 0.4 <-ACT g L752 0.4
L205 PE MATMUL X<-xT,w_in_sb 64*128 64x512 bf16 x512 | 63.1, 376 | 0.3 <-ACT r L741 0.2
```

The second half did not: every wait in the sum was one that the trace of before shows, and the new order made others: from 40 to 82 alone 11.1 us more were lost, where the sum has -0.7.

**The dense stage, -0.7.** From 40 to 82, 11.1 us more were lost. Three parts of that are shown, though they overlap and don't add: code that comes late (h1_shift; with loads cut, 70 to 82 loses 0.1 to 1.9), half clock behind the longest stop (some 1.7 us for 3.4 at 0.50), and waits for VectorE's normalize steps and casts. That full DMA queues make the code late is read from the shares and from these cut loads; no run takes that load away alone over the whole stretch. Taking one part away wins little or nothing: e3 against after, g3 against e4, h4 against h2. That the next is then met at nearly the same time is my reading of it. The prediction had read a few microseconds named "issue" in the trace of before, and took those at line 653 for the price of changing halves; that was not tested apart.

**The start, 0 (bounds -1.5 and +3).** Before 40 us 1.3 was lost, inside the bounds. But "Until batch 0's attention is done ScalarE sets the pace" holds in the new order to 40 us only: ScalarE has 14.14 of 15 from 25 to 40 and 22.29 of 30 from 40 to 70, and VectorE, with the table's steps, the mask casts, key gathers and casts all between 37 and 60, is what batch 0's last outputs and batch 1's queries wait for.

**The register loads, -1.4.** The direction held: the waits of 0.38 and 1.02 are gone, and 82 to 150 lost 5.2 less, more than register loads, visits and outputs together were to give there. Which of the causes gave the rest was not separated.

**Visits, -1.1 and +1.2.** The sum of the two was about right for 82 to 150 and too low behind: 150 to 225 lost 3.3 more, and 3.9 to 8.3 in all from kernel to kernel (f4_dmaout aside), 5.0 and 8.3 in two that run the same work there (g1_nops, h1_shift). No single stop of the kernel after there is over 0.75 us. That cause stays open.

**Transposes, -0.8, and the rival by which they were hidden.** In the new order they are not hidden: back on DMA, queries and keys cost 6.6 us of span and outputs 27.6 (against e1_stores, of another group).

**"Start and end stay."** The end is 3.5 us longer, all but 0.2 of it by one word of the order (e1_stores). The prediction had not read SyncE's last words of the new list.

**The late gathers of batch 1** were given 17% as the way to be slower. The sign and the place were near, the mechanism was not: no wait names `VG` there, and the stop of 0.65 at the first visit is a border of the code.

**Nothing moves**, the other rival, had 263.1. Much moved: 19.2 us were lost anew (11.1 + 3.5 + 3.3 + 1.3) and 5.7 won (5.2 from 82 to 150, 0.5 behind 225); that makes, but for rounding, the 13.6 between the two sums of lost time.

What stays open: how the 10 to 13 us that every version loses from 25 to 70 (18 in f3_dmaqk; 3.2 before) divide among the three parts, and what of them is neither. No version tried beats the kernel before.
